# Retention, then mixture of depths: the outputs' layout on DRAM, the order of the stores, and the loads of one step

## The chip, the cores and the metric

The kernel runs on one core of a Trainium2 chip. A core has five engines that run side by side, each with its own queue of instructions: TensorE (PE in the profile; PEld are its weight loads) multiplies matrices and writes to PSUM; VectorE (DVE) and ScalarE (ACT) work on elements and move results from PSUM to SBUF; GpSimd (POOL) works on elements in SBUF and here issues the indirect transfers; SyncE (SP) issues the plain transfers. Engines wait for each other, and for transfers, through semaphores. Transfers run on 16 DMA engines that all queues share.

The metric is the device time of one execution in microseconds; the median of the runs is compared. The kernel before takes 259.64 us (median of 14 runs, 257.13 to 263.7).

## The reference

Two blocks follow each other, all in float32, with B = 8 batches, H = 8 heads, S = 576 tokens, head size 64, so D = 512, hidden size F = 1024, and capacity 128:

```python
scores = scale * np.matmul(q, k.transpose(0, 1, 3, 2))
ret = scores * Dmat[None, :, :, :]          # gamma_h ** (i - j) for i >= j, else 0
attn_out = np.matmul(ret, v)
x = attn_out.transpose(0, 2, 1, 3).reshape(B, S, H * D)

scores = np.einsum('bsd,d->bs', x, w_gate)
out = x.copy()
for b in range(B):
    top_idx = np.argpartition(-scores[b], capacity)[:capacity]
    xe = x[b, top_idx]
    h = np.maximum(xe @ w1, 0.0)
    ye = h @ w2
    g = 1.0 / (1.0 + np.exp(-scores[b, top_idx]))
    out[b, top_idx] = x[b, top_idx] + g[:, None] * ye
```

So each batch has a retention block over all its tokens, a choice of the 128 tokens with the highest gate score, and an MLP on those tokens alone, whose result is written over their rows.

## The kernel before

**Tiling.** A sequence is cut into NC = 9 chunks of C = 64 tokens. A *step* s takes two chunks (`chunk(s, 0)` and `chunk(s, 1)`, which may belong to two batches: in steps 4, 13, 22 and 31); there are NS = 36 steps, 4.5 per batch. Four heads lie in the upper 64 partitions and four in the lower ones (`halves`), so a tile of 128 partitions by 512 holds two chunks of all heads: columns 0 to 255 (W = 256) the first chunk, 256 to 511 the second.

**Retention in a step.** `load` (L99) brings 1 MB of q, k, v and k again into `raw[s]`. `scaled` (L186, on POOL, L188) makes `vs[s]`, the values times a decay. TensorE's `diagonal` makes the state updates `u_ps` (they read `vs[s]`) and the scores `sc_ps`; DVE masks the scores to `am` (L261). In the step after, `crosswise` makes the values `y_ps`, and `values` (L265) scales them to `xs[s]` on ACT or DVE and takes each token's gate score (L292). `matmuls(s)` (L247) weaves `diagonal(s)` and `crosswise(s - 1)` together in 16 rounds of four matmuls; `inner` plants other work at a round: `plan(inner, (s, i), f)` puts f ahead of round i of step s.

**Stores.** `stored(s)` (L295) writes `xs[s]` to `outs[b]`, a DRAM tensor of S rows by 512. A row's two halves of heads lie in different halves of the partitions, so a step takes two transfers of 64 partitions (L300), four in a step of two batches (L304, L305). The dictionary `stores` (L500) says by step which earlier steps are stored: nothing before step 5, then steps 0 to 3 at once, step 4 in step 6, none in steps 7 and 8, and so on; from step 12 on step s - 2.

**The choice of tokens and the MLP.** `flatten`, `spread` and `compare` rank the scores of a batch; `one_hot` and `fetch` (L377) turn the ranks into 128 row numbers `idx[b]`, by a matmul of a one-hot matrix with the table `place` of row numbers. `fetch` then gathers these rows from `outs[b]` into `xr[b]` by an indirect transfer on POOL (L385); it must wait for the batch's stores. `turn` (L400) transposes `xr` on TensorE (L404), `up` and `down` are the MLP's two halves in four parts each (`h_ps` and `ye_ps` in the profile); the last part of `down` adds `xr` and scatters the rows back by an indirect transfer on POOL (L429). `gates` makes the sigmoid. `parts` is a list of MLP parts that wait; each step does some of them (`some`), so that a batch's MLP is spread over the next batch's retention.

**Order.** `manual_schedule` keeps the order in which the program issues, for each engine. For SP this means that a store waits behind all loads issued before it. Loads are not issued freely: `pe` (L113) counts TensorE's instructions, and each time the count passes an edge of 256, `start` issues due weights and one load, tied to that matmul. `due` says by step when each of eight weight pieces (four of w1, four of w2) may go; two loads go at the edges of steps 4 and 6 (L127); with `quiet`, set by a fetch, one edge is skipped.

**Where it hangs for the first batch.** Its last chunk is in step 4. `fetch(0)` is planted in step 7 at round 5 (L472), `mlp(0)`, that is `turn(0)` and then its parts, in step 9 at round 6 (L473), the first part in step 9 at round 15 (L474).

Of the kernel before, what the change touches and what calls it, by code (L numbers as in the profile page):

```python
# [17 lines left out]
P = 128  # L18
TINY = 2.0**-125
C = 64  # L20
# [7 lines left out]
def layout(NC, HG, cap):  # L28

    at, n = {}, 0  # L30
    for name, size in (("dec", 2 * (NC + 1) * HG), ("causal", C), ("ident", C), ("gate", HG * C),
                       ("slots", cap), ("eye", P), ("place", -(-NC * C // P))):
        at[name] = n
        n += size
    at["end"] = n
    return at
# [3 lines left out]
def kernel(  # L40
# [25 lines left out]
    DM = outs[0].shape[1]  # L66
# [46 lines left out]
    def pe(ins, n=4):  # L113

        now["at"] += n
        if now["at"] >= now["edge"] + SURE:
            now["edge"] += BLOCK
            lead = now["load"] - now["step"]
            if now["quiet"] and lead > 2:
                now["quiet"] -= 1  # L120
                return ins
            for _ in range(1 + (now["step"] > 7)):
                if weights and weights[0][0] <= now["step"]:
                    start(*weights.popleft()[1:], ins)

            ranks = (NC - 1) // 2 <= now["step"] < (NC - 1) // 2 + 3
            for _ in range(1 + (now["step"] in ((NC - 1) // 2, (NC - 1) // 2 + 2))):  # L127
                if now["load"] < NS and now["load"] - now["step"] < 4 + ranks:
                    load(ins)
        return ins  # L130
# [17 lines left out]
    w1_sb = const.tile([P, KD, F], F32, name="w1_sb")  # L148
    w2_sb = const.tile([P, FB, DM], F32, name="w2_sb")
    due = 5, 8, 8, 9, 9, 10, 10, 11  # L150
    assert FB == 8
    for i in range(FB // 2):
        e = slice(2 * P * i, 2 * P * i + 2 * P)
        weights.append((due[i], w1_sb[:, :, e], w1[i].rearrange("p (a f) -> p a f", a=KD)))
# [10 lines left out]
    place = const.tile([P, NJ], F16, name="place")  # L165
# [99 lines left out]
    def values(s):  # L265
        xs[s] = work.tile([P, DM], F32, name="xs", bufs=9)
# [28 lines left out]
    def stored(s):  # L295
        (b, c), (b1, _) = chunk(s, 0), chunk(s, 1)
        for i, half in enumerate(halves):
            e = slice(W * i, W * i + W)
            if b == b1:
                nc.sync.dma_start(  # L300
                    out=outs[b][C * c : C * c + P, e].rearrange("(a t) e -> t a e", a=2),
                    in_=xs[s][half, :].rearrange("p (a e) -> p a e", a=2))
                continue
            nc.sync.dma_start(out=outs[b][C * c :, e], in_=xs[s][half, :W])  # L304
            nc.sync.dma_start(out=outs[b1][:C, e], in_=xs[s][half, W:])  # L305
# [71 lines left out]
    def fetch(b):  # L377
        t = bank("idx_ps")
        for j in range(NJ):
            n = min(P, S - P * j)  # L380
            matmul(t[:, :1], hot[b][:n, j, :], place[:n, j : j + 1], start=j == 0, stop=j == NJ - 1)
        idx[b] = work.tile([P, 1], I32, name="idx", bufs=6)
        nc.scalar.copy(out=idx[b], in_=t[:, :1])
        xr[b] = work.tile([P, DM], F32, name="xr", bufs=6)
        nc.gpsimd.indirect_dma_start(  # L385
            out=xr[b], out_offset=None, in_=outs[b],
            in_offset=bass.IndirectOffsetOnAxis(ap=idx[b][:, :1], axis=0))
        now["quiet"] = 1
# [18 lines left out]
    def up(b, f, n):  # L407
        if f == 0:
            hT[b] = work.tile([P, FB, P], F32, name="hT", bufs=2)
        need(f // 2)  # L410
        t = bank("h_ps").rearrange("p (a e) -> p a e", a=4)
        for a in range(n):
            for d in range(KD):
                matmul(t[:, a, :], w1_sb[:, d, P * (f + a) : P * (f + a) + P],
                                 xg[b][:, d, :], start=d == 0, stop=d == KD - 1)
        nc.scalar.activation(out=hT[b][:, f : f + n, :], in_=t[:, :n, :], func=AF.Relu)  # L416

    def down(b, part):
        if part == 0:
            ye[b] = bank("ye_ps")  # L420
        need(FB // 2 + part)
        n = FB // 4
        for f in range(n * part, n * part + n):
            matmul(ye[b], hT[b][:, f, :], w2_sb[:, f, :], start=f == 0, stop=f == FB - 1)
        if part < 3:
            return
        o = work.tile([P, DM], F32, name="o")
        nc.vector.scalar_tensor_tensor(o, ye[b], gate[b], xr[b], op0=OP.mult, op1=OP.add)  # L428
        nc.gpsimd.indirect_dma_start(  # L429
            out=outs[b], out_offset=bass.IndirectOffsetOnAxis(ap=idx[b][:, :1], axis=0),  # L430
            in_=o, in_offset=None)
# [17 lines left out]
    for b in range(B):  # L449
# [15 lines left out]
        if b == 0:  # L465
# [7 lines left out]
            plan(inner, (s + 4, 6), mlp, b)  # L473
            plan(inner, (s + 4, 15), some, 1)  # L474
# [18 lines left out]
        if b < B - 2:  # L493
# [3 lines left out]


    FETCH = (NC - 1) // 2 + 3
    stores = {4: [], 5: [0, 1, 2, 3], 6: [4], FETCH: [], FETCH + 1: [], FETCH + 2: [5, 6],  # L500
              FETCH + 3: [7, 8], FETCH + 4: [9]}
# [3 lines left out]
    for s in range(NS + 1):  # L505
# [7 lines left out]
        for r in stores.get(s, [s - 2] if s > FETCH + 4 else []):  # L513
            stored(r)
# [14 lines left out]
        n = 1 if s == FETCH + 2 else n  # L529
# [87 lines left out]
```

## Time and profile before

| what | before |
|---|---|
| median of 14 runs | 259.64 us |
| the profiled execution's own time | 254.8 us |
| its span in the trace | 253.1 us |
| TensorE's granted clock, mean | 0.947 |
| plain transfers on SP's queue | 52.02 MB, 61.8% of 16 engines' span |
| indirect transfers on POOL's queue | 4.20 MB, 5.1% |
| gathers L385, issue to landing, median of 8 | 4.8 us |
| scatters L429, issue to landing, median of 8 | 4.1 us |
| loads of 1 MB, issue to landing, median | 7.3 us |
| stores of 128 KB (64 of them), median | 6.3 us |

The span is the time from the first to the last instruction that the trace holds. In what follows, "landing" is the moment when a transfer's semaphore reached its full count. The page cuts the span into 40 slices of 6.3 us and gives for each the busy share of each engine in tenths, and the clock that TensorE was granted. A line of the timeline has start, duration, engine, line, operation, tiles (out<-in) and, in brackets, how long the engine stood idle before and what ended that. In the chain that ended last each line has start, duration and the work on it.

### The profile page before, as it was taken

How to read it: one execution, taken by the hardware profiler on the slowest of the kernel's cores; microseconds unless marked ns; L12 is line 12 of the kernel's file. 1: busy time of each engine (PE TensorE's matmuls, PEld its weight loads, DVE VectorE, ACT ScalarE, POOL GpSimd, SP SyncE). 2: the span in 40 equal slices, each digit the busy share in tenths (PEclk: the TensorE clock that was granted, in tenths of full speed). 3: DMA queues.
4: the chain of work that ended last, by engine and by line, in shares of the span. 5: the costliest groups of instructions: out<-in, count | busy, mean ns of one | idle time of the engine just before them, and what ended most of it. 6: DMA issues, size and time to landing. Idle time of an engine off the chain costs nothing.

```text
span 253.1 us, 11383 instructions
## 1 busy us (share of the span) xinstructions
PE 224.9 (89%) x5104; PEld 176.0 (70%) x5104; DVE 155.1 (61%) x444; ACT 60.6 (24%) x183; POOL 58.9 (23%) x59
## 2 busy tenths in 40 slices
PE   8656667588988999999999989999999999999990
PEld 3555557478955799677985789669966986874940
DVE  0154994527399668969956597479954973931101
ACT  2146343015310232132121312123212220220200
POOL 3332410510114113242233303314141210101101
PEclk9999955559999999999999999999999999999997
DMA  6888999589998889877888657789977131201101
GB/s 208 356 313 282 345 313 353 174 332 273 412 409 264 232 272 310 277 249 225 253 252 267 209 186 220 241 285 280 294 261 262 54 76 49 75 10 41 44 0 43
DMA packets 20273, 56.95 MB, mean 225 GB/s; under 512 B 2304, under 2 KB 13696, under 8 KB 15744
## 3 DMA queue, kind: packets, MB, share of 16 engines
q1 hardware_dynamic: 18944, 52.02, 61.8%
q0 software_dynamic: 1280, 4.20, 5.1%
q8 instruction: 40, 0.66, 1.1%
q14 instruction: 9, 0.07, 0.1%
HBM read 44.67 MB, written 11.53 MB: 222 GB/s over the span
## 4 chain that ended last, share of the span: by engine, by line
PE 50%; issue 21%; DMA 17%; DVE 4%; POOL 3%; SPq 2%; ACT 1%; POOLq 1%
PE h_ps L137 14%; PE ye_ps L137 12%; DMA raw<-in_qkvk 9%; PE u_ps L137 8%; PE sc_ps L137 7%; DMA out<-xs 7%; PE y_ps L137 6%; PE row_ps L137 2%; DMA xr<-out,idx 2%; DVE scr L360 2%; POOL vs L188 1%; PE xg_ps L404 1%; SPq L305 1%; DVE scr L292 1%; POOL xr L385 1%
## 5 line engine op out<-in xcount | busy, mean ns | idle before, releaser
L188 POOL TENSOR_TENSOR vs<-raw,table 128x512 f32<-128x512 f32 x36 | 39.5, 1098 | 96.5 <-DMA raw<-in_qkvk 79.4
L137 PE MATMUL h_ps<-xg,w_sb 128*128 128x128 f32 x512 | 61.2, 278 | 0.0
L137 PEld LDWEIGHTS h_ps<-xg,w_sb 128*128 128x128 f32 x512 | 58.8, 192 | 2.2 <-issue 1.0
L137 PE MATMUL ye_ps<-w_sb,hT 128*128 128x512 f32 x128 | 60.2, 605 | 0.0
L137 PE MATMUL u_ps<-vs,raw 64*64 64x64 f32 x1024 | 46.1, 230 | 12.0 <-POOL vs L188 9.1
L137 PEld LDWEIGHTS u_ps<-vs,raw 64*64 64x64 f32 x1024 | 38.3, 142 | 20.8 <-POOL vs L188 10.8
L137 PE MATMUL sc_ps<-raw 64*64 64x64 f32 x1152 | 45.9, 229 | 2.4 <-issue 1.3
L261 DVE TENSOR_TENSOR am<-sc_ps,table 128x512 f32<-128x512 f32 x36 | 24.8, 689 | 37.5 <-PE sc_ps L137 22.5
L137 PE MATMUL y_ps<-vs,am 64*64 64x64 f32 x1152 | 46.5, 230 | 0.7 <-issue 0.5
L137 PEld LDWEIGHTS sc_ps<-raw 64*64 64x64 f32 x1152 | 41.1, 143 | 5.2 <-issue 2.8
L292 DVE SCALAR_TENSOR_TENSOR scr<-xs,table 128x256 f32<-128x256 f32 x72 | 38.3, 532 | 8.4 <-ACT xs L277 6.2
L137 PE MATMUL y_ps<-st,raw 64*64 64x64 f32 x1024 | 41.0, 230 | 1.1 <-issue 1.1
L208 ACT COPY st<-u_ps 128x256 f32<-128x256 f32 x64 | 23.9, 374 | 75.6 <-PE u_ps L137 48.4
L137 PEld LDWEIGHTS y_ps<-vs,am 64*64 64x64 f32 x1152 | 40.0, 141 | 1.7 <-issue 1.4
L360 DVE SCALAR_TENSOR_TENSOR scr<-row,tok,ahead 128x576 f32<-128x576 f32 (+5 forms) x52 | 37.3, 717 | 2.9 <-ACT row L336 0.8
L137 PEld LDWEIGHTS y_ps<-st,raw 64*64 64x64 f32 x1024 | 37.2, 145 | 1.4 <-issue 1.3
L137 PEld LDWEIGHTS ye_ps<-w_sb,hT 128*128 128x128 f32 x128 | 22.7, 189 | 21.4 <-issue 20.1
L280 DVE TENSOR_TENSOR xs<-y_ps,table 128x512 f32<-128x512 f32 x30 | 20.4, 681 | 8.1 <-PE y_ps L137 8.1
L416 ACT ACTIVATE hT<-h_ps 128x256 f32<-128x256 f32 x32 | 12.3, 384 | 49.8 <-PE h_ps L137 49.8
L428 DVE SCALAR_TENSOR_TENSOR o<-ye_ps,gate,xr 128x512 f32<-128x512 f32 x8 | 6.0, 748 | 25.8 <-PE ye_ps L137 13.1
L429 POOL DMA_INDIRECT out<-o,idx x8 | 8.6, 1071 | 50.9 <-DVE o L428 39.9
L353 DVE SCALAR_TENSOR_TENSOR scr<-row,table 128x128 f32<-128x128 f32 (+1 forms) x40 | 13.3, 333 | 9.8 <-ACT row L336 9.1
(33 smaller groups left out, 109.2 us busy)
## 6 DMA issues: line engine op xcount, KB each, us to landing
raw<-in_qkvk SPq DMA_DIRECT2D x35, 1024.0 KB, 7.3
out<-xs SPq DMA_DIRECT2D x64, 128.0 KB, 6.3
w_sb<-in_w SPq DMA_DIRECT2D x8, 512.0 KB, 5.5
raw<-in_qkvk SPq DMA_DIRECT2D x2, 512.0 KB
out<-xs SPq DMA_DIRECT2D x16, 64.0 KB, 5.2
table<-in_consts SPq DMA_DIRECT2D x1, 258.5 KB, 7.5
wg<-in_w_gate SPq DMA_DIRECT2D x1, 256.0 KB, 6.7
xr<-out,idx POOLq DMA_INDIRECT x8, 4.8
```

The lines of the kernel that those rows point to most:

```text
L137: return pe(nc.tensor.matmul(out, lhsT, rhs, **more), 4 if lhsT.dtype == F32 else 2)
L188: nc.gpsimd.tensor_tensor(out=four(vs[s]), in0=four(raw[s][:, 2, :]), in1=factor(s, 0), op=OP.mult)
L208: nc.scalar.copy(out=st[b, c], in_=u_ps[b][:, :W])
L261: nc.vector.tensor_tensor(out=am[s], in0=sc_ps[s].rearrange("p (h d) -> p h d", h=H), in1=causal.unsqueeze(1).to_broadcast([P, H, C]), op= ...
L280: nc.vector.tensor_tensor(out=four(xs[s]), in0=four(y_ps[s]), in1=factor(s, 1), op=OP.mult)
L292: nc.vector.scalar_tensor_tensor(scr[:, :W], part, 1.0, wg_half, op0=OP.mult, op1=OP.mult, accum_out=sc[b][:, c : c + 1])
L305: nc.sync.dma_start(out=outs[b1][:C, e], in_=xs[s][half, W:])
L353: nc.vector.scalar_tensor_tensor(scr[:, :n], row[b][:, P * j : P * j + n], 1.0, eye[:, :n], op0=OP.mult, op1=OP.mult, accum_out=tok[b][:, ...
L360: nc.vector.scalar_tensor_tensor(scr[:, : i1 - i0], row[b][:, i0:i1], tok[b][:, j : j + 1], ahead[:, at + i0 : at + i1], op0=OP.subtract, ...
L416: nc.scalar.activation(out=hT[b][:, f : f + n, :], in_=t[:, :n, :], func=AF.Relu)
L428: nc.vector.scalar_tensor_tensor(o, ye[b], gate[b], xr[b], op0=OP.mult, op1=OP.add)
L429: nc.gpsimd.indirect_dma_start(out=outs[b], out_offset=bass.IndirectOffsetOnAxis(ap=idx[b][:, :1], axis=0), in_=o, in_offset=None)
```

## The change

Five things change together.

1. `outs[b]` is now 2S rows by 256: for each chunk first 64 rows of one half of the heads, then 64 of the other. A step's `xs` goes to it in one transfer of 128 partitions, or in two when it has two batches. The host puts the halves together. `place` holds two row numbers per token, `fetch` makes two columns of `idx` and gathers each half in an indirect transfer of its own; `down` likewise scatters in two.
2. The dictionary `stores` is gone: step s stores step s - 2, from step 2 on. `xs` has 6 buffers for 9.
3. Step 6's edge issues one load and one piece of weights, for two loads (`due` 5, 6, 8 ... for 5, 8, 8 ...; L127), and the edge of step 8 one piece of weights for two.
4. `mlp(0)` moves from step 9, round 6, to step 8, round 14; its first part from round 15 of step 9 to round 5. Step 8 then does no part at its end.
5. w1 lies in SBUF by piece, so that a piece is contiguous in a partition; and the last batch's `down` makes the two halves of its columns one after the other, each with its own matmuls of 256 columns, its own `o` and its own scatter.

```diff
-            for _ in range(1 + (now["step"] > 7)):
+            for _ in range(1 + (now["step"] > 8)):
                 if weights and weights[0][0] <= now["step"]:
                     start(*weights.popleft()[1:], ins)
...
-            for _ in range(1 + (now["step"] in ((NC - 1) // 2, (NC - 1) // 2 + 2))):
+            for _ in range(1 + (now["step"] == (NC - 1) // 2)):
                 if now["load"] < NS and now["load"] - now["step"] < 4 + ranks:
                     load(ins)
...
-    w1_sb = const.tile([P, KD, F], F32, name="w1_sb")
+    w1_sb = const.tile([P, FB // 2, KD, 2 * P], F32, name="w1_sb")
...
-    due = 5, 8, 8, 9, 9, 10, 10, 11
+    due = 5, 6, 8, 9, 9, 10, 10, 11
...
-        xs[s] = work.tile([P, DM], F32, name="xs", bufs=9)
+        xs[s] = work.tile([P, DM], F32, name="xs", bufs=6)
...
-        for i, half in enumerate(halves):
-            e = slice(W * i, W * i + W)
-            if b == b1:
-                nc.sync.dma_start(
-                    out=outs[b][C * c : C * c + P, e].rearrange("(a t) e -> t a e", a=2),
-                    in_=xs[s][half, :].rearrange("p (a e) -> p a e", a=2))
-                continue
-            nc.sync.dma_start(out=outs[b][C * c :, e], in_=xs[s][half, :W])
-            nc.sync.dma_start(out=outs[b1][:C, e], in_=xs[s][half, W:])
+        if b == b1:
+            nc.sync.dma_start(out=outs[b][P * c : P * c + 2 * P, :].rearrange("(a p) e -> p a e", a=2),
+                              in_=xs[s].rearrange("p (a e) -> p a e", a=2))
+            return
+        nc.sync.dma_start(out=outs[b][P * c :, :], in_=xs[s][:, :W])
+        nc.sync.dma_start(out=outs[b1][:P, :], in_=xs[s][:, W:])
...
-            matmul(t[:, :1], hot[b][:n, j, :], place[:n, j : j + 1], start=j == 0, stop=j == NJ - 1)
-        idx[b] = work.tile([P, 1], I32, name="idx", bufs=6)
-        nc.scalar.copy(out=idx[b], in_=t[:, :1])
+            matmul(t[:, :2], hot[b][:n, j, :], place[:n, 2 * j : 2 * j + 2], start=j == 0,
+                   stop=j == NJ - 1)
+        idx[b] = work.tile([P, 2], I32, name="idx", bufs=6)
+        nc.scalar.copy(out=idx[b], in_=t[:, :2])
         xr[b] = work.tile([P, DM], F32, name="xr", bufs=6)
-        nc.gpsimd.indirect_dma_start(
-            out=xr[b], out_offset=None, in_=outs[b],
-            in_offset=bass.IndirectOffsetOnAxis(ap=idx[b][:, :1], axis=0))
+        for i in range(2):
+            nc.gpsimd.indirect_dma_start(
+                out=xr[b][:, W * i : W * i + W], out_offset=None, in_=outs[b],
+                in_offset=bass.IndirectOffsetOnAxis(ap=idx[b][:, i : i + 1], axis=0))
...
+        cols, n = (2, FB // 2) if b == B - 1 else (1, FB // 4)
+        half, part = divmod(part, 4 // cols)
+        w = DM // cols
+        e = slice(w * half, w * half + w)
...
-        o = work.tile([P, DM], F32, name="o")
-        nc.vector.scalar_tensor_tensor(o, ye[b], gate[b], xr[b], op0=OP.mult, op1=OP.add)
-        nc.gpsimd.indirect_dma_start(
-            out=outs[b], out_offset=bass.IndirectOffsetOnAxis(ap=idx[b][:, :1], axis=0),
-            in_=o, in_offset=None)
+        o = work.tile([P, w], F32, name="o")
+        nc.vector.scalar_tensor_tensor(o, ye[b][:, :w], gate[b], xr[b][:, e], op0=OP.mult,
+                                       op1=OP.add)
+        for i in range(2 // cols):
+            nc.gpsimd.indirect_dma_start(
+                out=outs[b], out_offset=bass.IndirectOffsetOnAxis(
+                    ap=idx[b][:, half + i : half + i + 1], axis=0),
+                in_=o[:, W * i : W * i + W], in_offset=None)
...
-            plan(inner, (s + 4, 6), mlp, b)
-            plan(inner, (s + 4, 15), some, 1)
+            plan(inner, (s + 3, 14), mlp, b)
+            plan(inner, (s + 4, 5), some, 1)
...
-    stores = {4: [], 5: [0, 1, 2, 3], 6: [4], FETCH: [], FETCH + 1: [], FETCH + 2: [5, 6],
-              FETCH + 3: [7, 8], FETCH + 4: [9]}
...
-        for r in stores.get(s, [s - 2] if s > FETCH + 4 else []):
-            stored(r)
+        if s > 1:
+            stored(s - 2)
...
-        n = 1 if s == FETCH + 2 else n
+        n = max(0, s - FETCH - 1) if FETCH < s < FETCH + 3 else n
...
-    outs = [nc.dram_tensor(f"out_{b}", (S, DM), F32, kind="ExternalOutput").ap() for b in range(B)]
+    outs = [nc.dram_tensor(f"out_{b}", (2 * S, DM // 2), F32, kind="ExternalOutput").ap() for b in range(B)]
...
-    return np.stack([r.results[0][f"out_{b}"] for b in range(B)])
+    got = np.stack([r.results[0][f"out_{b}"] for b in range(B)])
+    return np.ascontiguousarray(
+        got.reshape(B, NC, 2, C, DM // 2).transpose(0, 1, 3, 2, 4).reshape(B, S, DM))
```

## The prediction

> **What bounds the kernel now.** I read the busy table and the slices of the page first, then the busy times by stage, then the chain that ended last, and last POOL's timeline with the landings of its transfers.
>
> ```profile
> PE 224.9 (89%) x5104; PEld 176.0 (70%) x5104; DVE 155.1 (61%) x444; ACT 60.6 (24%) x183; POOL 58.9 (23%) x59
> ...
> PE   8656667588988999999999989999999999999990
> ...
> PEclk9999955559999999999999999999999999999997
> ```
>
> TensorE has gaps only in the first 13 slices (80 us); in slices 6 to 9 its clock is halved. The busy times by stage (length, then each engine, then clock, DMA share, GB/s) say it in microseconds:
>
> ```profile
> 0.00:30.00 30.00, 20.24 (x703) 15.21 (x707) 11.87 (x37) 10.97 (x38) 10.25 (x14) 1.00 0.82 298
> 30.00:55.00 25.00, 16.02 (x473) 14.44 (x466) 15.15 (x48) 7.17 (x29) 5.27 (x5) 0.54 0.88 302
> 55.00:80.00 25.00, 22.55 (x585) 18.35 (x577) 17.50 (x46) 6.72 (x17) 5.18 (x5) 0.99 0.98 341
> 80.00:205.00 125.00, 123.90 (x3090) 98.84 (x3088) 95.68 (x268) 29.70 (x83) 32.87 (x30) 1.00 0.76 240
> ```
>
> From 80 to 205 us TensorE works 123.9 of 125 us: a wait put on it there is paid in full. Before that the kernel is held by the start of the first batch's MLP, as the chain shows:
>
> ```profile
> 39.05 7.30 DMA out<-xs
> 46.47 0.65 issue
> 47.17 0.08 issue
> 47.35 4.74 DMA xr<-out,idx
> 52.14 1.11 PE xg_ps L404 x4
> ```
>
> The last store of batch 0 leaves at 39.05 behind two 1 MB loads and eight deferred stores, the gather can start only at 47.35, and the transposes (L404) come at 52.14. The gather's indices had been there since 39.65 (end of the cast L383 in the timeline).
>
> **The start: earlier stores, `stores` removed, order of step 6, turn in step 8.** Steps 0 to 3 are now stored in steps 2 to 5 and step 4's two stores stand behind one load and one weight. The indices hang on DVE, which is busy without a break from 28.4 to 39.35, so they stay at 39.65. If step 4's stores have landed by then (they leave some 4 us earlier), the pair of gathers starts near 40.2 (0.5 us for POOL's chain of semaphores, as the 0.65 in the chain), the second 1.05 us later (mean of L385), and lands 4.74 us on: 46.0. TensorE transposes 6.1 us earlier, but the turn moves from the 7th of 16 rounds of step 9 to the 15th of step 8, so half a step is still to do behind it: 1.2 us at full clock (step 2 took 2.39 us, 13.73 to 16.12), 2.4 at half. Gain 6.1 - 1.8, about 4.0 with a little lost to early stores. Bounds: the gather can't start before 39.65, which is 6.6 us of gain without any remainder; on the other side three early stores, if each delays a load by a quarter of the 5.06 us that a load took alone (11.38 to 16.45), lose 3.9. I take **-4.0**, from the nearer row: DMA share is 0.66 to 0.85 between 12 and 22 us, so there is room for 0.25 MB a step.
>
> **The writes back: one becomes two, and the second waits.** A row of the output is now two rows of `outs[b]`, so each batch's gather and scatter are two indirect DMAs. In the instruction order of the changed kernel the two gathers follow each other freely, but the second scatter of each pair waits for the semaphore of the first: both write the same tensor at addresses known only at run time. POOL runs in order, so the wait holds what is queued behind: `vs` of a step (L188), whose first user is the `u_ps` matmul that opens that step on TensorE. Order there is unchanged from step 10 on. POOL's timeline before, start and duration:
>
> ```profile
> 87.43 1.04 POOL L429 DMA_INDIRECT out<-o,idx  x1 [5.69 <-DVE o L428]
> 88.50 1.06 POOL L188 TENSOR_TENSOR vs<-raw,table 128x512 f32<-128x512 f32 x1
> ...
> 118.78 1.03 POOL L429 DMA_INDIRECT out<-o,idx  x1 [4.10 <-DVE scr L353]
> 120.28 1.39 POOL L188 TENSOR_TENSOR vs<-raw,table 128x512 f32<-128x512 f32 x1 [0.47 <-DMA raw<-in_qkvk]
> ```
>
> The landing of the second of these, from the list of DMA issues between 118.5 and 120 us, and its user in TensorE's timeline:
>
> ```profile
> raw<-in_qkvk SPq DMA_DIRECT2D x1, 1024.0 KB, 8.0
> ...
> out<-o,idx POOLq DMA_INDIRECT x1, 8.4
> ```
> ```profile
> 124.49 0.23 PE L137 MATMUL u_ps<-vs,raw 64*64 64x64 f32 x2
> ```
>
> Five scatters have a `vs` behind them. They start at 87.43, 118.78, 142.24, 172.01 and 195.86 and land after 9.0, 8.4, 4.3, 7.9 and 2.8 us; the long three each have a 1 MB load issued within 0.5 us. TensorE's first use of the `vs` behind each comes at 93.37, 124.49, 148.65, 177.73 and 203.26: 5.94, 5.71, 6.41, 5.72 and 7.40 us after the scatter's start. After the change that `vs` ends a landing + 1.04 (second scatter) + 1.05 (`vs`) + 0.1 (hand-overs) after that start, so TensorE stands still for landing + 2.2 less those distances. The loads hang on the same matmuls as before, so the overlap should return; for half the bytes I take the shortest of the overlapped rows, 7.9, for all three: 4.1 + 4.3 + 0.1 + 4.3 + 0 = **+12.8**. Bounds: the rows themselves give 5.3 + 4.9 + 0.1 + 4.5 = 14.8; landings of the last three scatters, without loads (2.8 to 3.9), give at most 0.4 each, 1.0 in all.
>
> Each such stall also risks the clock. It stood at 0.50 from 32 to 54 us, after gaps of 0.57 and 1.40 us, and was full from 56 on, some 3 us after dense work began at 52.14. If a stall of 4 us halves it until 3 us of work have passed, 1.5 us are lost: 4.5 for three. But the longest gap at full clock, 2.38 us at 23.5, was not followed by a halving at once; so between 0 and 4.5 I take **+2.3**.
>
> Two rules of the Trainium skill stand against these rows. "DMA: Bandwidth & Descriptors", section on the SWDGE path, fits a transfer of this kind with about 2.0 us plus bytes over 436 GB/s; an estimate from it for 128 KB is 2.3 us, by which no stall would arise and the sum would be the start and the tail alone, -3.4. The trace's 9.0, 8.4 and 7.9 us for 256 KB contradict it wherever a load is in the rings. "TensorE: Matmul & The Clock Gate", Part 1, has the clock halved after an idle window of about 3.4 us and back after a busy one of that length; by it three stalls cost about 1.7 each, 5.1 instead of 2.3.
>
> **The tail.** The last gather's second half starts 1.0 later; TensorE waited 0.23 us for it at 231.02 already, and its first half serves two of the four transposes meanwhile: +0.9 at most, 0 if half the bytes land that much sooner; I take +0.8. The last `ye` in two halves has the same columns; `o` is 128x256 at the end, 0.53 (L292's mean for that size) instead of 0.75: -0.2. **+0.6.**
>
> **Costed at nothing.** Seven second gathers, 1.05 us of POOL each: the `vs` behind them had 2 us or more to its use (after 77.61: ends 79.68, used 81.94) or was waiting for a load anyway (after 130.11: 1.95), and xr landed 2.7 us or more before its transposes (114.42 against 117.11); uncovered, 7.4 at most. One load fewer ahead: POOL waited 79.4 us for raw, TensorE 9.1 for `vs`, all of it before 50 us, and from step 20 before too had only load s+2 in step s; uncovered, up to the wait of one load, 7.3 us median from issue, at the steps with weights. Stores in one transfer: the same 256 runs of 1 KB; SP's issues, 0.6 us each, halve, behind TensorE. Contiguous w1: earlier than its use. Fewer xs buffers: the store of step s-6 is four steps old.
>
> **Sum.** -4.0 + 12.8 + 2.3 + 0.6 = +11.7 on the profiled execution's 254.8 us (span 253.1): 266.5. The median shown is 4.8 above that execution; the difference carries over: 259.64 + 11.7 = **271.3**.
>
> **Rivals.** (a) Faster: the second scatter's wait stays covered and the start's gain is kept, 259.64 - 4.0 + 0.6 = 256.2. For it: two of the five landings, 2.8 and 4.3 us, cost nothing. Against: the other three, each with a load beside it. It decides from the first scatter's landing: below 3.5 us no stall is left, and from 4.7 on at three places (1.2 each) the gain is spent. (b) Partial overlap, three landings near 5 us: 1.4 x 3 + 0.6 - 4.0, near 260.5; the rings hold fewer stores at a time, yet the loads stay. (c) The early stores delay the loads of steps 4 to 6: the change then doesn't do at the start what it says, +3.9 instead of -4.0, 279. For it: a load's landing opens each of these steps (POOL waits at 12.63, 16.51, 20.58). Against: the DMA share there.
>
> **How the numbers follow.** Forecast 0.70, (a) 0.15, (b) 0.07, (c) 0.08. The likeliest one's own range goes from 264 (landings of 6.5 us, no clock loss) to 277 (the rows' own stalls, full clock loss, start gain 3). Over all, 256 to 278 leaves out half of (a), most of (c) and little else. About 0.5%, 1.3 us, is what can be told from no change here: slower by more has 0.70 + 0.08 + 0.02 of (b), 0.80; within 0.05; faster 0.15.
>
> **What would show it.** Right: POOL's second write of a pair begins only when the first landed, `u_ps` on TensorE idles about 4 us behind `vs` near 94, 125 and 178 us of the old count, and the slices there fall below 9; the transposes of batch 0 near 46 to 48 us. Wrong: first writes landing in 3 us, or TensorE without gaps from 80 on; or transposes later than 50 us, which would strike out the start's gain.

## The result, and the profile after

| | before | after |
|---|---|---|
| median of the runs | 259.11 us (47 runs, 254.78 to 266.11) | 272.87 us (10 runs, 267.8 to 281.24) |
| ratio after / before, 95% interval | | 1.0473, 1.0418 to 1.0528 |
| profiled execution | 254.8 us | 273.06 us |
| its span | 253.1 us | 271.3 us |

The kernel became slower by 4.7%. The 272.87 us lie 1.6 us above the predicted 271.3. Ratios leave disturbed executions out on both sides and so aren't quite the quotients of the medians. The two profiled executions differ by 18.2 us of span, more than the 13.8 us between the medians: that of before lies near the fast end of its runs, that of after in the middle of its own. What follows splits up the 18.2, and the part that is chance has to lie in there too.

The page of after, the lines that answer to those shown of before:

```profile
PE 231.0 (85%) x5120; PEld 183.4 (68%) x5120; DVE 156.6 (58%) x445; ACT 60.7 (22%) x183; POOL 73.7 (27%) x75
...
PE   8674767698888869969599999999599999998992
...
PEclk9999755579999999999979999999889999999998
```

Before, the digits of PE were 9 from the 14th slice (80 us) to the last but one, with one 8. Now there are falls in the 15th, 18th, 20th and 29th slice (6.8 us each), and the clock is down in the 21st and in the 29th and 30th, right behind the two deepest. The fall in the 18th belongs to a late load, the other three to writes back. The busy times of the same long stretch (length, then engines, clock, DMA share, GB/s):

```profile
80.00:205.00 125.00, 111.09 (x2770) 89.14 (x2763) 87.48 (x235) 26.07 (x72) 40.25 (x39) 0.97 0.70 227
```

TensorE worked 111.1 of these 125 us, where it had worked 123.9. The waits between 80 and 222 us (us in total, how often, the longest) name both ends of what is missing:

```profile
POOL out L434 <- DMA out<-o,idx: 23.3, 5, 6.3
...
PE u_ps L137 <- POOL vs L187: 13.8, 6, 3.5
```

Five times POOL stood at the second scatter of a pair (L434) for the landing of the first; six times TensorE stood at the first `u_ps` of a step for its `vs` (L187): three times behind such a pair (2.62, 3.51 and 3.29 us) and three times behind a late load (1.00, 1.08 and 2.25 us). The place for the first pair, in POOL's timeline (start, duration, the idle time before and what ended it), and TensorE's next line after it:

```profile
90.67 1.04 POOL L434 DMA_INDIRECT out<-o,idx  x1 [0.16 <-issue]
97.97 0.98 POOL L434 DMA_INDIRECT out<-o,idx  x1 [6.26 <-DMA out<-o,idx]
98.98 2.04 POOL L187 TENSOR_TENSOR vs<-raw,table 128x512 f32<-128x512 f32 x2
```
```profile
100.09 0.27 PE L137 MATMUL u_ps<-vs,raw 64*64 64x64 f32 x2 [2.62 <-POOL vs L187]
...
136.25 0.27 PE L137 MATMUL u_ps<-vs,raw 64*64 64x64 f32 x2 [3.51 <-POOL vs L187]
...
193.96 0.27 PE L137 MATMUL u_ps<-vs,raw 64*64 64x64 f32 x2 [3.29 <-POOL vs L187]
```

The first scatter landed 7.04 us after its start, at 97.71; the second began 0.26 later, and `vs` of step 16 ended at 100.03, 0.06 before its user. The other two lines are the same place behind the second and the fourth pair, whose first writes took 7.03 and 6.62 us. Behind the third pair (3.94 us) and the fifth (2.47) no gap of that kind stands.

At the start, the chain that ended last (start, duration, work) reads:

```profile
37.03 1.66 ACT xs L276 x8
38.69 0.02 issue
38.71 7.22 DMA out<-xs
45.93 0.01 issue
45.94 0.31 POOL xr L383
46.25 1.13 issue
47.38 4.76 DMA xr<-out,idx
52.15 0.04 issue
52.19 0.69 PE xg_ps L402 x2
```

Store, gather and transposes are still one behind the other, and the last transposes come at 52.19, where they had come at 52.14. The store left when the values it writes were ready (`xs`, 38.69), 0.34 us earlier than before, and nothing was gained by it here.

To see where each microsecond arises, I took from TensorE's timeline the start of the first `u_ps` of each step, and from it that of the same step in the profile of before (93.37 us for step 16, for instance, in the lines that the prediction shows). The columns e1 to e7 are experiments told of below; all but the first are differences in us:

| step | before, at | after | e1 | e2 | e6 | e7 |
|---|---|---|---|---|---|---|
| 10 | 59.72 | 1.94 | 3.83 | 3.62 | 2.31 | 0.75 |
| 15 | 86.30 | 4.27 | 5.78 | 2.99 | 2.05 | 4.04 |
| 16 | 93.37 | 6.71 | 5.54 | 7.94 | 2.02 | 5.56 |
| 21 | 117.47 | 8.08 | 9.70 | 8.61 | 3.34 | 7.21 |
| 23 | 129.49 | 13.38 | 9.66 | 11.88 | 3.31 | 7.00 |
| 30 | 170.73 | 12.76 | 9.15 | 11.09 | 2.55 | 6.75 |
| 32 | 183.37 | 17.88 | 9.15 | 16.22 | 2.55 | 6.75 |
| 35 | 203.26 | 18.02 | 9.26 | 16.39 | 2.74 | 6.92 |

In after, 1.9 us are there by step 10, 2.3 come between steps 10 and 15, 2.4 at step 16, 1.4 between 19 and 21, 5.3 from 21 to 23 and 5.1 from 30 to 32.

### The profile page after: what moved, and what is told of

It is laid out like the page before. It is cut to its first block, busy times and chain, and to the rows that moved or that the text cites. A ratio compares the mean times of both kernels' runs of the same rounds, so it can differ in the third digit from the quotient of the medians.

```text
span 271.3 us, 11395 instructions
## 1 busy us (share of the span) xinstructions
PE 231.0 (85%) x5120; PEld 183.4 (68%) x5120; DVE 156.6 (58%) x445; ACT 60.7 (22%) x183; POOL 73.7 (27%) x75
## 4 chain that ended last, share of the span: by engine, by line
PE 35%; DMA 26%; issue 22%; POOL 9%; DVE 4%; ACT 1%; SPq 1%; POOLq 1%; DVEq 0%
DMA raw<-in_qkvk 17%; PE h_ps L137 12%; PE ye_ps L137 6%; PE sc_ps L137 5%; PE u_ps L137 5%; DMA out<-xs 5%; PE y_ps L137 4%; POOL vs L187 4%; POOL out L434 3%; DMA xr<-out,idx 3%; PE row_ps L137 2%; DVE scr L291 2%; POOL xr L383 1%; ACT xs L276 1%; DMA out<-o,idx 1%
## 5 line engine op out<-in xcount | busy, mean ns | idle before, releaser
L137 PE MATMUL h_ps<-xg,w_sb 128*128 128x128 f32 x512 | 64.6, 287 | 0.0
L137 PEld LDWEIGHTS h_ps<-xg,w_sb 128*128 128x128 f32 x512 | 62.3, 202 | 2.4 <-issue 1.6
L187 POOL TENSOR_TENSOR vs<-raw,table 128x512 f32<-128x512 f32 x36 | 38.2, 1064 | 91.1 <-DMA raw<-in_qkvk 76.5
L137 PE MATMUL ye_ps<-w_sb,hT 128*128 128x512 f32 (+1 forms) x144 | 60.2, 556 | 0.0
L137 PEld LDWEIGHTS ye_ps<-w_sb,hT 128*128 128x128 f32 x144 | 25.7, 190 | 18.8 <-issue 16.7
L356 DVE SCALAR_TENSOR_TENSOR scr<-row,tok,ahead 128x576 f32<-128x576 f32 (+5 forms) x52 | 36.2, 695 | 2.9 <-ACT row L332 0.8
L434 POOL DMA_INDIRECT out<-o,idx x16 | 16.6, 1039 | 66.1 <-DVE o L431 34.3
L383 POOL DMA_INDIRECT xr<-out,idx x16 | 16.4, 1026 | 36.2 <-ACT idx L380 20.5
L431 DVE SCALAR_TENSOR_TENSOR o<-ye_ps,gate,xr 128x512 f32<-128x512 f32 (+1 forms) x9 | 6.2, 690 | 26.1 <-PE ye_ps L137 16.7
```

Of the source, the lines that this page charges most:

```text
L137: return pe(nc.tensor.matmul(out, lhsT, rhs, **more), 4 if lhsT.dtype == F32 else 2)
L187: nc.gpsimd.tensor_tensor(out=four(vs[s]), in0=four(raw[s][:, 2, :]), in1=factor(s, 0), op=OP.mult)
L356: nc.vector.scalar_tensor_tensor(scr[:, : i1 - i0], row[b][:, i0:i1], tok[b][:, j : j + 1], ahead[:, at + i0 : at + i1], op0=OP.subtract, ...
L383: nc.gpsimd.indirect_dma_start(out=xr[b][:, W * i : W * i + W], out_offset=None, in_=outs[b], in_offset=bass.IndirectOffsetOnAxis(ap=idx[b ...
L431: nc.vector.scalar_tensor_tensor(o, ye[b][:, :w], gate[b], xr[b][:, e], op0=OP.mult, op1=OP.add)
L434: nc.gpsimd.indirect_dma_start(out=outs[b], out_offset=bass.IndirectOffsetOnAxis(ap=idx[b][:, half + i : half + i + 1], axis=0), in_=o[:, ...
```

## The experiments

### The second scatter behind the next `vs`

After, with the second scatter of each of the five pairs inside the loop held back until the `vs` that stood behind it has been issued. Layout, bytes and number of transfers stay.

```diff
+    held = deque()
...
-            nc.gpsimd.indirect_dma_start(
+            if i and now["step"] < NS:
+                held.append((b, o, i))
+            else:
+                back(b, o, i, half)
...
             scaled(s + 2)
+        while held:
+            back(*held.popleft())
```

> The changed kernel with one thing moved: the second scatter of a pair is issued on POOL behind the next `vs` instead of ahead of it (five pairs; the last three are as they were). It still waits for the first to land, but nothing that TensorE needs stands behind it at once. Theory (the second scatter's wait costs TensorE its gaps): the gaps ahead of `u_ps` at the first, second and fourth of these pairs (2.6, 3.5 and 3.3 us in the profile of the changed kernel) and the halved clock behind two of them go, 9 to 13 us off, to 260 to 264. Rival (the time is lost by doubled gathers and by loads that come late, and scatters only happen to stand beside them): within 3 us of the changed kernel, 270 to 273.

Measured: 262.25 us (10 runs) against 260.23 of before on the same chip (13 runs), ratio 0.9948 (0.9749 to 1.0146). The 4.7% are not there any more: the interval reaches from 2.5% faster to 1.5% slower. On this same chip the kernels e3 and e4 below, which keep the wait, took 275.07 and 274.85 us. POOL's timeline at the first pair:

```profile
92.19 1.04 POOL L419 DMA_INDIRECT out<-o,idx  x1 [0.16 <-issue]
94.31 1.03 POOL L187 TENSOR_TENSOR vs<-raw,table 128x512 f32<-128x512 f32 x1 [1.09 <-PE y_ps L137]
97.69 1.02 POOL L419 DMA_INDIRECT out<-o,idx  x1 [2.34 <-DMA out<-o,idx]
```

`vs` now goes between the two writes and POOL's wait for the first landing holds nothing that TensorE needs soon. In the table the column e1 goes from 5.78 to 5.54 at step 16, from 9.70 to 9.66 between 21 and 23, and stays at 9.15 from 30 to 32: the three places where after and e2 jump. What this profile is late it had by step 21, some of it at the start, some where a load was late (at 119.70 `vs` of step 20 ended a wait of 3.00 us for `raw`, and TensorE stood 2.25 us for it).

### The wait alone, put into the kernel before

Before, each of the five scatters inside the loop preceded by a scatter of its first 64 rows (2 KB each: the 128 KB of a half). The rows are written twice with the same values.

```diff
-        nc.gpsimd.indirect_dma_start(
-            out=outs[b], out_offset=bass.IndirectOffsetOnAxis(ap=idx[b][:, :1], axis=0),
-            in_=o, in_offset=None)
+        for n in (C, P) if now["step"] < NS else (P,):
+            nc.gpsimd.indirect_dma_start(
+                out=outs[b], out_offset=bass.IndirectOffsetOnAxis(ap=idx[b][:n, :1], axis=0),
+                in_=o[:n, :], in_offset=None)
```

> The kernel before with one thing added: each of the five scatters that have a `vs` behind them is preceded by a scatter of its first 64 rows, so that POOL has two scatters into one tensor and the second waits for the first. Theory: as in the prediction, landing + 2.2 us less 5.9, 5.7, 6.4, 5.7 and 7.4, so 9 to 15 us slower than before, 268 to 275. Rival (half a scatter lands in 3 us also beside a load): 259 to 261.

Measured: 271.33 us (4 runs) against 260.23, ratio 1.0448 (1.0365 to 1.0530): the loss of the whole change, in a kernel with the old layout, the old stores and the old loads. The same picture as in after, from POOL's timeline and TensorE's:

```profile
90.43 0.95 POOL L430 DMA_INDIRECT out<-o,idx  x1 [5.02 <-DVE o L428]
99.18 1.00 POOL L430 DMA_INDIRECT out<-o,idx  x1 [7.80 <-DMA out<-o,idx]
100.20 2.05 POOL L188 TENSOR_TENSOR vs<-raw,table 128x512 f32<-128x512 f32 x2
```
```profile
101.31 0.37 PE L137 MATMUL u_ps<-vs,raw 64*64 64x64 f32 x2 [4.91 <-POOL vs L188]
```

The first write took 8.5 us to land and TensorE stood for 4.91. The kernel also has five more indirect transfers, but so has the deferred one, without a loss. The column e2 grows at the same three places as after and, like after, not at the pairs that landed after 3.7 and 2.6 us. It also shows 3.62 us by step 10, in a part of the program that is the same as in before: so much do two executions of one code differ at the start.

### The old stores, and the old loads

Two kernels undo one part of the order each, with the wait left in. The first takes the old dictionary of stores back:

```diff
-        xs[s] = work.tile([P, DM], F32, name="xs", bufs=6)
+        xs[s] = work.tile([P, DM], F32, name="xs", bufs=9)
...
+    stores = {4: [], 5: [0, 1, 2, 3], 6: [4], FETCH: [], FETCH + 1: [], FETCH + 2: [5, 6],
+              FETCH + 3: [7, 8], FETCH + 4: [9]}
...
-        if s > 1:
-            stored(s - 2)
+        for r in stores.get(s, [s - 2] if s > FETCH + 4 else []):
+            stored(r)
```

> The changed kernel with the old times of the stores (the dictionary `stores` and 9 buffers of xs), still one transfer a step. Theory (early stores stand in the way of the loads of steps 4 to 7): `vs` of step 6 is ready near 29 us again instead of 31.9, the first batch's indices near 39.7 instead of 42.5, but step 4's store then leaves behind four others; the first transposes move by 0 to -2 us: 0 to 3 us faster than the changed kernel. Rival (the early stores don't touch the loads; the late start is chance): `vs` of step 6 stays at 31 to 32 us, time within 1 us or slower.

Measured: 275.07 us (4 runs) against 260.23, ratio 1.0566 (1.0483 to 1.065), no faster than after. Its profile can't say what the early stores cost: it was 3.7 us late at step 3 already, before anything in it differs from before. From step 5 to step 6 it took 4.77 us, where before took 3.57, after 5.76 and e1 5.75, so early stores may cost a microsecond there; in the time it isn't seen. Inconclusive on the size, and against rival (c), by which the time should have fallen.

The second takes the old loads and weights back:

```diff
-            for _ in range(1 + (now["step"] > 8)):
+            for _ in range(1 + (now["step"] > 7)):
...
-            for _ in range(1 + (now["step"] == (NC - 1) // 2)):
+            for _ in range(1 + (now["step"] in ((NC - 1) // 2, (NC - 1) // 2 + 2))):
...
-    due = 5, 6, 8, 9, 9, 10, 10, 11
+    due = 5, 8, 8, 9, 9, 10, 10, 11
```

> The changed kernel with two loads at step 6's edge and the old due times of the weights. Theory (one load fewer ahead costs the waits for `vs` in steps 11 to 15, where TensorE lost 2.4 us between the first `u_ps` of step 11 and that of step 15 against before): these waits go, 2 to 3 us faster than the changed kernel. Rival (the doubled gathers on POOL make these waits): no difference beyond 1 us.

Measured: 274.85 us (4 runs), ratio 1.0537 (1.0419 to 1.0655). Between steps 11 and 15 its profile grows from 4.63 to 4.87, where after grows from 1.94 to 4.27: the loss there is one of the loads. But it began later (the transposes of batch 0 at 53.0 and 55.6 us) and its first scatter took 8.9 us to land, and the whole is not better than after.

### The deferred scatter with the old loads, then with the old order as a whole; the new order alone

Three kernels ran on one chip, side by side with before (259.65 us, 29 runs). The first is the deferred scatter with the loads of the diff above. The second has the deferred scatter and everything old but the layout (w1 by piece and the last batch's two halves also stay new):

```diff
-            plan(inner, (s + 3, 14), mlp, b)
-            plan(inner, (s + 4, 5), some, 1)
+            plan(inner, (s + 4, 6), mlp, b)
+            plan(inner, (s + 4, 15), some, 1)
...
-        n = max(0, s - FETCH - 1) if FETCH < s < FETCH + 3 else n
+        n = 1 if s == FETCH + 2 else n
```

with the two diffs of stores and loads on top. The third is the reverse, before with the new stores, loads, weights and turn, in the old layout with one scatter:

```diff
-        for r in stores.get(s, [s - 2] if s > FETCH + 4 else []):
-            stored(r)
+        if s > 1:
+            stored(s - 2)
...
-    due = 5, 8, 8, 9, 9, 10, 10, 11
+    due = 5, 6, 8, 9, 9, 10, 10, 11
...
-            plan(inner, (s + 4, 6), mlp, b)
-            plan(inner, (s + 4, 15), some, 1)
+            plan(inner, (s + 3, 14), mlp, b)
+            plan(inner, (s + 4, 5), some, 1)
```

> The changed kernel with the deferred second scatter and with two loads at step 6's edge and the old due times of the weights. Theory (with the scatters out of the way what is left over before is the start, 0 to +4 us by execution, and about 2 us of waits for `vs` in steps 11 to 15 by one load fewer ahead): no growth between the first `u_ps` of steps 11 and 15, 1 to 3 us faster than the deferred kernel, level with before within 1.5 us (258 to 262). Rival (the loads don't matter once POOL is free): as the deferred kernel, about 262.

> The new layout alone: the changed kernel with the deferred second scatter and with the old order of stores, loads, weights and of the first batch's turn. Theory (layout and doubled gathers cost next to nothing once the wait is out of the way; the new order at the start gains nothing): level with before within 1.5 us, 258 to 262. Rival (doubled gathers on POOL cost 1 us each at some batches): 263 to 266.

> The other half: the kernel before, its layout and single gathers and scatters kept, with the new order of stores, loads, weights and of the first batch's turn. What the prediction gave the start, -4.0 (the pair of gathers left out, -5 or so): 254 to 256. Theory after the first runs (the gather starts earlier after its indices, but the indices come later and half a step is left to do, so the start gives 0; one load fewer ahead costs 2): 259 to 263.

Measured, 12 runs each: 259.7 us, ratio 1.0059 (1.0013 to 1.0106); 257.91, ratio 0.9971 (0.9923 to 1.0019); 260.17, ratio 0.9971 (0.9915 to 1.0027). So without the wait the new layout costs nothing on this chip with the old order, and 0.6% with the new stores and turn; and the new order alone is worth nothing that can be told from zero: the start's 4 us are not in it. The growth between steps 11 and 15 goes with the loads once more: 1.37 to 4.04 in the third, none in the first (6.95 to 6.85) and the second (2.31 to 2.05).

### A load put back at step 9, and two of the kernels again

If the start's gain is real and fewer loads ahead eat it, a second load at the edge of step 9, past the hurry of the start, should bring it out. Two kernels have it: after with the deferred scatter, and the old layout with the new order.

```diff
-            for _ in range(1 + (now["step"] == (NC - 1) // 2)):
+            for _ in range(1 + (now["step"] in ((NC - 1) // 2, NC))):
```

Beside them ran the deferred scatter with the new order and with the old order, unchanged from above.

> The deferred kernel with one edit more: two loads at step 9's edge, so that from there on the loads run as far ahead as in the kernel before; stores, step 6 and the turn stay as changed. Theory A (the start does gain the 4 us of the prediction, and one load fewer ahead takes 5 to 6 back between steps 10 and 21, as two profiles with the new order show): the `u_ps` of steps 10 and 21 are equally far from before, and the time is 253 to 257. Theory B (the start gains nothing; differences at step 10 are chance): 258 to 261.

> The same in the old layout: the kernel before with the new order of stores, weights, step 6 and the turn, and with two loads at step 9's edge. Theory A: 3 to 5 us faster than the same kernel without those two loads (260.2), 254 to 257. Theory B: no difference, 259 to 261.

> The deferred kernel once more, as the neighbour of the first run of this call on the same chip. Both theories: 259 to 263; A wants it 4 or more slower than with two loads at step 9, B within 1.5.

> New layout, deferred scatter and the old order once more, to see whether its 0.3% against before holds: 257 to 259 if it does, 259 to 261 if it was chance. A wants it 2 to 4 slower than the first run of this call, B level or faster.

| kernel, on the third chip | median, us | ratio to before | interval |
|---|---|---|---|
| before (17 runs) | 267.48 | | |
| new layout, deferred, new order, load at step 9 (6) | 275.68 | 1.0485 | 1.039 to 1.058 |
| old layout, new order, load at step 9 (12) | 263.65 | 0.9976 | 0.9865 to 1.0087 |
| new layout, deferred, new order (6) | 274.23 | 1.0377 | 1.0224 to 1.0531 |
| new layout, deferred, old order (6) | 274.82 | 1.0294 | 1.0059 to 1.0528 |

The three kernels with the new layout are level with each other, so neither the order nor the load shows here. But all three lose against before, and on the chips of the earlier runs they had not (0.9948 and 0.9971 for the last two rows). The waits of TensorE between 80 and 222 us, for the last row's kernel on this chip, and for the same kernel in the earlier run:

```profile
PE y_ps L137 <- issue: 5.3, 13, 1.0
PE sc_ps L137 <- issue: 5.1, 8, 1.8
PE u_ps L137 <- issue: 0.4, 1, 0.4
```
```profile
PE y_ps L137 <- issue: 1.7, 3, 1.2
```

There is no wait for `vs` in either. On this chip 10.8 us stand under "issue", where TensorE waited for nothing that the profile shows; in the earlier run it was 1.7. TensorE's timeline around one such place (start, duration, idle before):

```profile
139.42 0.23 PE L137 MATMUL sc_ps<-raw 64*64 64x64 f32 x2
139.44 0.22 PE L137 MATMUL y_ps<-vs,am 64*64 64x64 f32 x1
139.82 0.21 PE L137 MATMUL y_ps<-vs,am 64*64 64x64 f32 x1 [0.17 <-issue]
139.84 0.36 PE L137 MATMUL sc_ps<-raw 64*64 64x64 f32 x4
140.58 0.30 PE L137 MATMUL y_ps<-vs,am 64*64 64x64 f32 x3 [0.38 <-issue]
141.32 0.21 PE L137 MATMUL y_ps<-vs,am 64*64 64x64 f32 x1 [0.44 <-issue]
```

Short bursts, then 0.4 us of nothing. By the same view they come to 7.7, 8.5 and 10.8 us in the three kernels with the new layout and to 4.4 in the one with the old layout, here; in the five kernels with a profile of this kind on the two earlier chips (e1, e4 to e7) to 1.2 to 2.6. POOL's timeline shows what they stand beside, a pair of gathers:

```profile
139.25 1.00 POOL L383 DMA_INDIRECT xr<-out,idx  x1 [4.03 <-DMA raw<-in_qkvk]
140.56 0.96 POOL L383 DMA_INDIRECT xr<-out,idx  x1 [0.31 <-issue]
```

It is so throughout. In the four profiles of this chip 81 of the 88 gaps under "issue" of more than 0.1 us, between 80 and 222 us, begin while POOL executes an indirect transfer or within 0.2 us of its end, though these transfers fill only 12 to 24 us of that stretch; in the other ten profiles it is none of 21. They come where TensorE runs matmuls of 64x64; beside `h_ps` alone there are none. The new layout has two transfers where the old has one: from the first `u_ps` of a step with gathers (19, 23, 28, 32) to that of the next step the three kernels with pairs lost 10.6, 13.5 and 10.6 us in all against the profile of before, the one with single gathers 3.8. That is 6.8, 9.7 and 6.8 more than with single gathers, of the 7.1, 10.6 and 11.1 us that part these profiles at step 35. The gaps are not all of it: in the kernel with 13.5, for instance, the clock is at 0.54 and 0.60 in the two stretches of 2 us from 140 us on, behind the gathers of step 23. So on this chip the doubled gathers were not free, and most of what the new layout loses there arises beside them. This is read from the profiles; no kernel took the pairs of gathers out of the new layout. Why TensorE stops beside an indirect transfer on this chip and in none of the other profiles stays open, and before was not profiled here.

### The parts that cost nothing, in the old layout

Old layout, new order, the load at step 9, and w1 by piece: all of the change that does not need two scatters.

```diff
-    w1_sb = const.tile([P, KD, F], F32, name="w1_sb")
+    w1_sb = const.tile([P, FB // 2, KD, 2 * P], F32, name="w1_sb")
...
-        e = slice(2 * P * i, 2 * P * i + 2 * P)
-        weights.append((due[i], w1_sb[:, :, e], w1[i].rearrange("p (a f) -> p a f", a=KD)))
+        weights.append((due[i], w1_sb[:, i, :, :], w1[i].rearrange("p (a f) -> p a f", a=KD)))
```

> What is left of the change when the layout goes, as a candidate: the old layout with single gathers and scatters, the new order of stores, weights, step 6 and the turn, two loads at step 9's edge, and contiguous pieces of w1. Theory (the whole loss lies in the second scatter's wait; the start is worth 1 to 2 us at most): ratio to before 0.985 to 1.000, TensorE without gaps behind `vs` of 2 us or more after 100 us. Rival (the new order itself costs time): ratio above 1.005.

Measured: 257.05 us (12 runs) against 257.62 on a fourth chip (17 runs), ratio 0.9969 (0.9923 to 1.0015). Level with before. No version that I tried is faster than before beyond its interval.

## Why the prediction was right, point by point

**The sign and the mechanism: right, and shown.** The second write of a pair waits for the landing of the first, POOL holds `vs` behind it, and TensorE stands. Putting `vs` ahead of that wait took the loss away (0.9948, where e3 and e4 on the same chip have 1.0566 and 1.0537), and the wait alone, in the kernel before, gave the loss (1.0448). The three signs named in advance are there: POOL's second write 0.26 us after the landing, `u_ps` idle at three places (2.6 to 3.5 us, for about 4), slices below 9. One reserve: on the third chip the deferred scatter did not bring the time back to before (1.0377), with no wait behind the scatters left; what was lost there stands beside the doubled indirect transfers. The scatters' wait explains the loss on the chips where it was taken out with success.

**Scatter waits, +12.8: right kind, mis-sized.** 2.4, 3.7, 0 and 3.5 us at steps 16, 22, 26 and 31, and nothing at 35: 9.6 in all. The rule "landing plus 2.2 less the distance to the user" stands. The landings of the halved writes were 7.04, 7.03 and 6.62 us, not 7.9, where the whole ones took 9.0, 8.4 and 7.9 before. That half the bytes land sooner isn't shown by this: in the other runs first writes of 128 KB at the first of these places took 5.2 to 9.1 us, and whole ones 6.8 to 9.3. And at the first pair TensorE was busy until 97.47, 6.8 us after the scatter's start where it had been 5.94.

**Clock, +2.3: between the bounds, measured near 3.3.** Behind the gaps of 3.51 and 3.29 us TensorE ran with a mean granted clock of 0.79 for 8 us, behind that of 2.62 with 1.00:

```profile
100.00:108.00 8.00, 7.91 (x273) 7.66 (x273) 6.71 (x19) 1.88 (x5) 1.70 (x3) 1.00 0.51 169
136.00:144.00 8.00, 7.75 (x158) 7.58 (x159) 1.55 (x5) 1.40 (x5) 1.70 (x3) 0.79 0.34 117
...
193.00:201.00 8.00, 7.04 (x83) 6.31 (x84) 4.33 (x17) 1.24 (x3) 1.90 (x2) 0.79 0.41 154
```

8 x 0.21 is 1.7 us each, and the table grows by 1.6 from step 22 to 23 and by 1.7 from 31 to 32. The rule that the prediction set against its own term ("TensorE: Matmul & The Clock Gate", Part 1, of the Trainium skill, the clock halved after an idle window of about 3.4 us) fits these three stalls one by one: the two near that length cost 1.7 us each, the shorter one nothing; its estimate of 5.1 counted three long ones. The length of a stall doesn't decide alone, though: behind the stall of 2.25 us in e1 the clock was at 0.57 from 121 to 125 us, and behind one of 3.06 us in e2 (at 136.33) it stayed full. The other rule ("DMA: Bandwidth & Descriptors", the fit for the SWDGE path, by estimate 2.3 us for 128 KB) fits the fifth pair, 2.47 us with no load issued beside it, and misses by 4.3 to 4.7 us at the three long ones.

**The start, -4.0: the step that failed.** In the profiled pair it is +1.9 by step 10, and the new order alone gives a ratio of 0.9971 with an interval on both sides of 1. Three parts of the working went wrong. The indices were said to stay at 39.65, since DVE is busy; they came at 42.55, in a profile whose step 6 was late (first `u_ps`: 31.99 for 29.43). The stores were said to leave some 4 us earlier and to have landed by then; the last was issued at 38.71, 0.34 us earlier than before, behind its own values, and landed at 45.93, and the gather started at 45.94. And the gather is now two: the second half started 1.44 us after the first and landed at 52.15, 3.3 after the first half's 48.84. TensorE transposed the first half at 48.96 and then stood 2.54 us for the other. So the "transposes later than 50 us" that the prediction named as striking out this gain hold for the second half. In the seven profiles with the new order step 10 lies -4.3 to 3.8 us from where it was in before, -0.1 in the mean; in the four with the old order 0 to 3.6, 1.9 in the mean. A gain of 4 is not there as a rule; one of 2 at step 10 may be, is smaller than this scatter, and the timed kernels don't show it.

**"One load fewer ahead", costed at nothing: wrong, by 2 to 4 us in the profile.** The growth between steps 11 and 15 is 2.3 in after, 2.0 in e1 and 2.7 in e7, and 0.2, -0.1 and -0.3 in e4, e5 and e6 with the old loads (e11, with the old loads on the third chip, grew by 2.9, behind gaps of the kind found there). Another 1.4 come between steps 19 and 21: `vs` of step 20 waited 2.55 us for its load and TensorE stood 2.25 at 121.18. Not all of that is the loads': in e4 to e6, with the old ones, 0.7 to 0.8 come there too, behind a gap of 1.2 us named "issue". The prediction had looked at waits of TensorE for `vs` after 50 us, 0 in before, and taken the lead for spare; it was what kept them at 0. In the times it is too small to be seen by itself: 259.7 and 260.17 us with and without the old loads, in two layouts.

**Seven second gathers, costed at nothing: held in this profile, not on the third chip.** The pair ahead of `vs` of step 20 is the one where a `u_ps` came late, and there POOL was done with the second gather and idle before the load landed:

```profile
116.32 0.96 POOL L383 DMA_INDIRECT xr<-out,idx  x1 [0.30 <-issue]
119.83 1.30 POOL L187 TENSOR_TENSOR vs<-raw,table 128x512 f32<-128x512 f32 x1 [2.55 <-DMA raw<-in_qkvk]
```

On the third chip the price was paid on TensorE and not on POOL, in the gaps told of above, a path that the prediction didn't look at.

**Tail, +0.6:** +0.2 from the first `u_ps` of step 35 to the end of the span.

**The sum.** -4.0 + 12.8 + 2.3 + 0.6 = 11.7 was forecast. Measured in the profiled pair: 1.9 (start) + 2.3 and 1.4 (loads) + 9.6 (scatters) + 3.3 (clock) + 0.2 (tail) - 0.5, which came back between steps 23 and 35: 18.2. Between the medians it is 13.8. The total was good partly because errors cancelled: too much for the waits, too little for the loads and the clock, and a gain at the start that did not come, against a profile of before that lay 4.3 us under its median and so made the pair look worse than the kernels are. Two bounds were also added up wrongly, without weight for the forecast: the fourth term of 14.8 is 4.4 and not 4.5 (7.9 + 2.2 - 5.72), and landings of 6.5 us without clock loss give 265 and not 264.

**The rivals.** (a), covered waits, fell with landings of 6.6 to 7.0 us, far above its point of 3.5. (b), landings near 5 us, fell with them. (c), early stores delaying loads: the first load behind them took longer (`vs` of step 6 ready at 31.94 for 29.13), so the mechanism exists: from the first `u_ps` of step 5 to that of step 6 the nine profiles with early stores took 5.0 to 6.3 us, the five with the old stores 3.6 to 5.3. But taking the early stores out did not make the kernel faster; it is a microsecond or so.

## What to carry to other kernels

When one indirect write becomes two to the same tensor, the second costs not its own microsecond but the landing of the first, and that is read from the landings beside the loads of the same stage, not from the transfer's size; look at what stands behind it on the queue, and put that in between before anything else. The doubled issue can also have a price on an engine that doesn't take part, as TensorE's gaps on the third chip show, so time such a change on more than one chip. A transfer that is moved forward gains only up to the next thing that is late, so list all that the following step needs (here indices, the store's landing and both halves of the gather) and expect the last of them. And where one code moves by 3 us from one execution to the next, a pair of profiles shows where a wait arises, but its size has to come from timed kernels that differ in that wait alone.

## What the runs showed of the hardware that was not expected

A scatter of 128 KB landed 2.5 us after its start with no load issued beside it, and 6.6 to 7.0 us (in other runs up to 9.2) beside a 1 MB load; one of 256 KB took 2.8 and up to 9.3. What shares the rings counts for more than the bytes, and so does the order: over all profiles, scatters with the next load issued 0.29 to 0.71 us behind their start landed after 5.2 to 8.5 us, those with it 0.96 or 0.97 us behind after 3.2 to 5.0. The third scatter of before (4.3 us) is of the second kind: it has a load beside it too, only later.

An indirect transfer of 128 rows mostly occupied POOL for 0.96 to 1.13 us with rows of 1 KB as with rows of 2 KB, and one of 64 rows of 2 KB for 0.95: cutting rows in two doubles that price.

The kernel before had medians of 259.65, 260.23, 257.62 and 267.48 us on four chips. On the slowest of them TensorE stood 4 to 11 us in gaps of mostly 0.4 us, nearly all begun beside an indirect transfer on POOL; in the profiles from elsewhere no gap began there. What was level with before on two chips (0.9948, 0.9971) lost 3 to 4% on this one.
